# Row halves and marks for the down products and the output projection in the last sections of an attention and gated feed-forward kernel

## The chip, the cores and the metric

The kernel runs on one core of one Trainium2 chip. The metric is the device time of one execution in microseconds (us); of several executions the median is taken. The kernel before takes 2547.48 us, the median of 3 runs from 2546.96 to 2547.53 us.

## The reference

The input is 2048 tokens of width 576. With `xn` the layer norm of `x`, two branches are computed from `xn`: a 32-head attention (18 numbers a head) with its output projection `wo`, and a feed-forward branch with 4608 hidden values. They meet in the last line.

```python
x = A_x
xn = _layernorm(x, axis=-1)
s = _A_ref(xn, A_wqkv, A_wo)                     # softmax(q k^T) v, then @ wo
g = _silu(_B_ref(xn, B_w_gate, B_w_up, B_w_down))  # (gelu(xn @ w_gate) * (xn @ w_up)) @ w_down
return x + s * g
```

All arrays are 32-bit floats. The kernel splits every operand of a large product into a high and a low part and adds three products of parts (high by high, high by low, low by high).

## The kernel before, in words

**The whole.** A first stage norms `x`, transposes it and computes queries, keys and values. Then come 144 sections. One section computes 128 hidden values for 512 tokens: `gate_up` (L400 to L416) runs 27 pairs of products, and in each pair the gate product uses the rows 0 to 63 of the TensorE array (PE) and the up product the rows 64 to 127, at the same time. Two sections (g = 0 and 1) make one round r of 18; four blocks b of 512 tokens make 72 rounds. The sections 10 to 137 carry the attention between their products. The sections 138 to 143, which the loop variable of L939 counts as n = 128 to 133, belong to the last block (b = 3, rounds 15 to 17). They have no attention left; beside the feed-forward branch they carry the output projection. They are the place of the change.

**A last section, in PE's order.** PE's order is the order in which the program is written; it is not rearranged. First the 27 pairs of `gate_up`. Then the down products of half a round (`down`, L512): for two groups of 128 tokens (j) and two halves of the 576 columns (c), that is four sums, six products each (`DOWN`, L458), 128 rows deep and 288 columns wide. Then, for n = 129 to 132, the output projection of three places (a place is a block b and a group j, 16 in all): `project_o` (L899) makes two sums a place, 14 products each (`OUT`, L933), so 84 products. The last section, n = 133, has no projection in its loop body; two places follow at L986, then the down products of round 17, then the last two places.

**What the other engines do in a last section.** `activate` (L424): ScalarE (ACT) squares the gate sum (L426), VectorE (DVE) makes the inner part of the gelu (L427). `run_rest` (L554) then calls `rest` (L436): tanh on ACT (L437) and two products on DVE (L440, L444) that read the gate and up sums out of PSUM. `add_down` (L448) adds a finished down sum to `Y` in SBUF (DVE, L453). For every place, `gate_place` (L895) computes tanh on ACT (L420) and a product over 576 columns on DVE (L421); the tile `th` between them has one buffer. `put` (L905) multiplies a finished projection sum by the gate (L909, reads PSUM) and adds `x` (L910), both on DVE. `finish` (L566) with `cut` splits the hidden values and, when g is 1, the down weights: the high part on ACT (L116), the low part on DVE (L117). `prepare(p)` (L920) has GpSimd (POOL) split the attention output of place p into `oh` and `ol` (L106, L108) with a cast of 64 rows (L882), and loads `x` and the stored sums of that place. `AHEAD` is 3: the parts of place p use the buffers of place p - 3. POOL also splits the gate and up weights of the next section.

**What sets the order.** PSUM has eight banks in three groups: `BANKS` gives two to "f", three to "m" and three to "s". A sum holds one bank until it has been read. `gate_up` takes two of "f" or two of "m" in turn. The down sums and the projection sums of the last sections take "s" one after another. `kept` (L397) pins an instruction behind whatever instruction was written last for the same engine; from n = 128 on nearly all work of ACT, DVE, POOL and SyncE (SP) is pinned so. In the last sections the order on DVE is: L427, four `add_down`, L440, L444, then place by place gate and puts, with `finish` behind the second place.

**Halves and marks, as they stand.** In the attention sections `half_downs` (L474) runs a whole round of eight down sums in row halves: every product is two products of 64 rows, one for each half of the array, side by side. The two halves of one sum may not write its bank at the same time, so one half begins with the last two sums and the other with the first, and each sum changes halves: `behind` (L468) writes a one-column "mark" on ACT which waits for the last product of the first half, and the first product of the other half waits for the mark. `FF["rest"]` is then called from inside `half_downs`, behind a mark:

```python
if begun == 0 and i == 0 and k in seen:
    after(one, seen[k])
...
    seen[k] = behind(one)
    if k in (0, late) and FF["rest"]:
        FF["rest"].pop(0)(seen[k], evicted if k == 2 else None)
```

Of the kernel before, what the change touches and what calls it, by code (L numbers as in the profile page):

```python
# [8 lines left out]
F32 = mybir.dt.float32  # L9
# [8 lines left out]
P = 128  # L18
# [3 lines left out]
KT = 4  # L22
# [47 lines left out]
def kernel(ctx: ExitStack, tc: tile.TileContext, x, wqkv, wo, w_gate, w_up, w_down, out):  # L70
# [34 lines left out]
    def split(hi, lo, raw, keep=lambda i: i):  # L105
        first = nc.gpsimd.tensor_scalar(hi, raw, 1.0, 1.0, op0=ALU.mult, op1=ALU.mult)  # L106
        keep(first)
        low_part[:] = [keep(nc.gpsimd.tensor_tensor(lo, raw, f(hi), op=ALU.subtract))]  # L108
        return first
# [287 lines left out]
    def kept(i):  # L397

        if FF["keep"]:
            tc.keep_in_program_order(i)  # L400
        return i
# [58 lines left out]
    def bank(tag):  # L460
        return ps.tile([P, 288], F32, name="py", tag=tag, bufs=BANKS[tag])
# [9 lines left out]
        after(it, one)  # L471
        return it

    def half_downs(b, r, hs, wd, Y):  # L474

        m = len(DOWN)
        sums = [(j, c) for j in range(TB // P) for c in range(2)]
        low = len(sums) - 2  # L480
        pys, seen, evicted = {}, {}, None
        late = 2 if r == NR - 1 else 1

        def downs_of(a, ks):
            for k in ks:
                for i in range(m):
                    def step(k=k, i=i):
                        nonlocal evicted
                        j, c = sums[k]
                        fresh = k not in pys  # L490
                        if fresh:
                            pys[k] = bank("mmsmfmss"[k])
                        begun = a if k < low else 1 - a
                        one = down_product(pys[k], hs, wd, j, c, i, slice(HR * a, HR * a + HR), fresh,
                                           begun == 0 and i == m - 1)
                        if begun == 0 and i == 0 and k in seen:
                            after(one, seen[k])
                        if i == m - 1:
                            if begun == 0:
                                evicted = add_down(b, r, pys[k], Y, j, c)  # L500
                            elif a == 1:
                                seen[k] = behind(one)
                                if k in (0, late) and FF["rest"]:
                                    FF["rest"].pop(0)(seen[k], evicted if k == 2 else None)
                    yield step

        n = range(len(sums))
        rows = [*downs_of(0, n[low:]), *downs_of(0, n[:low])], [*downs_of(1, n)]
        for i, both in enumerate(zip(*rows, strict=True)):
            for half in both if i < low * m + m else both[::-1]:  # L510
                half()

    def down(b, r, hs, wd, Y, js, once):
        last = len(DOWN) - 1
        if once:
            if js[0] == 0:
                half_downs(b, r, hs, wd, Y)
        else:
            for j in js:
                for c in range(2):  # L520
                    py = bank("sf"[c if b == NB - 1 and r == NR - 1 else 0])
                    for i in range(len(DOWN)):
                        down_product(py, hs, wd, j, c, i, start=(i == 0), stop=(i == last))
                    add_down(b, r, py, Y, j, c)
        if b < NB - 1 and r == NR - 1:
            for j in js:
                kept(nc.sync.dma_start(ys[b * TB + j * P:b * TB + (j + 1) * P, :], Y[:, j]))
# [104 lines left out]
    def load_wo(i):  # L632

        for w, c, k in ((w, c, k) for w in range(2) for c in range(2) for k in range(NK)):
            if i != (5 + k // 3 if w and c else k) or (c and not w):
                continue
            n, wide = min(P, D - k * P), D if not w else 288
            to, cc = f(flat[i]), slice(288 * c, 288 * c + wide)
            o = D if w and not c else 288 * (k % 3) if w else 0
            for a in range(1 if w or n == P else 2):  # L640
                kept(nc.sync.dma_start(to[HR * a:HR * a + n, o:o + wide], wos[w, k * P:k * P + n, cc]))
            if w and n < P:
                kept(nc.gpsimd.memset(to[HR:P, o:o + wide], 0.0))

    with tc.tile_pool(name="att", bufs=1, reuse_waits="tile") as att:
# [211 lines left out]
    with tc.tile_pool(name="epi", bufs=1, reuse_waits="tile") as epi:  # L857
# [20 lines left out]
        def split_o(b, j):  # L878

            oh, ol = parts_of(b, j)  # L880
            split(oh, ol, OT[b % 2][:, :, j * P:(j + 1) * P], kept)
            kept(nc.gpsimd.tensor_copy(oh[HR:P, KT, :], ol[0:HR, KT, :]))  # L882

        def row_tile(name):
# [14 lines left out]
        def project_o(b, j, c, tag):  # L899
            po = ps.tile([P, TB], F32, name="po", tag=tag, bufs=BANKS[tag])[:, 0:288]  # L900
            for i, (k, x_, w) in enumerate(OUT):
                nc.tensor.matmul(po, parts_of(b, j)[x_][:, k, :], OW[w][c][k], start=(i == 0), stop=(i == len(OUT) - 1))  # L902
            return po

        def put(b, j, c, po, add):  # L905

            cc = slice(288 * c, 288 * c + 288)
            xx, yy = XY[b, j]
            kept(nc.vector.scalar_tensor_tensor(yy[:, cc], yy[:, cc], 0.25, po, op0=ALU.mult, op1=ALU.mult))  # L909
            kept(add.tensor_tensor(yy[:, cc], yy[:, cc], xx[:, cc], op=ALU.add))  # L910
            if c or b == NB - 1:
                cc = cc if b == NB - 1 else slice(0, D)
                kept(nc.sync.dma_start(out[b * TB + j * P:b * TB + (j + 1) * P, cc], yy[:, cc]))
# [6 lines left out]
        def prepare(p):  # L920

            if p < len(places):
                b, j = places[p]
                split_o(b, j)
                load_xy(b, j)
                if j == 0 and 0 < b < NB - 1:
                    load_o(b + 1)
# [10 lines left out]
        for n in range(NU * NA, ENDS):  # L938
            first, last = n == NU * NA, n == ENDS - 1  # L939
            if first:  # L940
                rec = epi.tile([P, D], F32, name="th")[:, 0:TB]
                tc.keep_in_program_order(nc.vector.reciprocal(rec, SUM))
            section([], "m" if n % 2 else "f", ahead=first)
            if first:
                FF["keep"] = True
                load_wo((n - 1) % KB)
                load_o(0)
                for o in OT:
                    kept(nc.gpsimd.memset(o[HR:P, KT, :], 0.0))
                prepare(0)  # L950
                prepare(1)
                next_weights(n)
                prepare(2)
                where = [(u % NQ, slice(S - TB, S)) for u in range(NU - 2, NU)]
                store_sums(*where[1])
                kept(nc.sync.dma_start(rT[H - QD:H, S - TB:S], rec.rearrange("(a p) t -> a p t", p=32)[:, 0, :]))
                pieces = [(S3[0:QD * DH, 0:TB], ffn.tile([P, TB], F32, name="t2", bufs=1)[0:QD * DH]),
                          [row_tile(m)[0:QD * DH, 0:TB] for m in ("xx", "yy")]]
                for piece, to in zip(pieces, where):
                    load_numbers(*piece, *to)  # L960
                load_o(1)
            else:
                next_weights(n)
                for k in range(0 if last else NG - 1):
                    split_gu(FF["w"], k, kept)
            downs()
            run_rest()
            if first or last:
                finish(epi, cut, 2)
            else:  # L970
                for i in range(3):
                    b, j = places[done]
                    if b < NB - 1:
                        gate_place(b, j)
                    for c in range(2):
                        put(b, j, c, project_o(b, j, c, "s"), nc.vector)
                    done += 1
                    if i == 0:
                        split_gu(FF["w"], NG - 1, kept)
                    prepare(done - 1 + AHEAD)  # L980
                    if i == 1:
                        finish(epi, cut, 2)
                    if done == 2:
                        for piece, to in zip(pieces, where):
                            norm_numbers(*piece, *to, nc.vector)
        for b, j in places[done:done + 2]:  # L986
            for c in range(2):
                kept(nc.scalar.activation(SS[2 * j + c], project_o(b, j, c, "s"), AF.Copy))
            done += 1
            prepare(done - 1 + AHEAD)  # L990
# [51 lines left out]
```

## Time and profile before

| what | value |
|---|---|
| time, median of 3 runs | 2547.48 us |
| span of the profiled execution, first to last instruction | 2545.4 us |
| busy: PE / DVE / ACT / POOL | 2538.4 / 1950.4 / 1555.1 / 1320.7 us |
| granted TensorE clock, mean | 1.000 |

One execution was profiled, and its own time is the span; the median of the runs is 2.08 us above it. Times in the views count from the first instruction. A row of a timeline has the start, the duration (merged rows: of all together), engine, line, operation, output and inputs, and how many instructions stand in it; in brackets the idle time before and what ended it. "64\*128 64x288" is a product of 64 rows by 288 columns in one half of the array; "x2" with that shape is a pair side by side. The chain of work that ended last lists start, duration and work without gaps. Matmuls overlap in the records: the rate is seen in the distance of their starts, not in their durations.

### The profile page before, as it was taken

The page shows a single profiled execution, that of the slowest core. Times are in us where ns is not written, and L with a number is a line of the kernel's source. Part 1 is how long each engine was busy: PE and PEld are TensorE (multiplying, and loading weights), DVE is VectorE, ACT ScalarE, POOL GpSimd, SP SyncE. Part 2 cuts the span into 40 slices and gives each one's busy share as a digit, 9 for nine tenths or more (in the row PEclk, how much of TensorE's full clock was granted, in tenths as well). Part 3 has the DMA queues.
Part 4 walks back from the last instruction along what each step waited for, and adds up shares of the span by engine and source line. Part 5 has one row for each costly group of instructions (what it writes and reads, how often), then busy time and mean ns, then how long its engine had stood idle before and what let it go on. Part 6 is the DMA issues. An engine that isn't in the chain of part 4 may idle for free.

```text
span 2545.4 us, 63167 instructions
## 1 busy us (share of the span) xinstructions
PE 2538.4 (100%) x23974; PEld 2008.4 (79%) x23974; DVE 1950.4 (77%) x3499; ACT 1555.1 (61%) x3050; POOL 1320.7 (52%) x1447
## 2 busy tenths in 40 slices
PE   9999999999999999999999999999999999999999
PEld 8888877777777777777777787777777777787798
DVE  5316988888888888888888888888888888887277
ACT  3223366666677666676666677666676666676612
POOL 2117545555465554445565545554446555455675
PEclk9999999999999999999999999999999999999999
DMA  8876444444465444444455444444446444444483
GB/s 267 269 241 158 100 103 106 100 111 109 107 150 121 104 109 112 113 112 110 111 125 140 116 111 106 105 108 112 109 109 153 115 109 109 108 106 99 114 242 107
DMA packets 398686, 325.51 MB, mean 128 GB/s; under 512 B 117408, under 2 KB 309184, under 8 KB 398384
## 3 DMA queue, kind: packets, MB, share of 16 engines
q1 hardware_dynamic: 398384, 321.47, 49.7%
q8 instruction: 191, 3.13, 0.5%
q14 instruction: 111, 0.91, 0.1%
HBM read 266.63 MB, written 54.70 MB: 126 GB/s over the span
## 4 chain that ended last, share of the span: by engine, by line
PE 98%; ACT 1%; DVE 0%; DMA 0%; SPq 0%; issue 0%; ACTq 0%
PE pg L413 29%; PE py L465 18%; PE acc L764 18%; PE pm L698 9%; PE pe L729 9%; PE po L180 7%; PE pu L413 6%; PE po L902 2%; ACT pT L730 1%; PE pt L241 0%; SPq L665 0%; DMA xx<-in_A_x_dram 0%; DVE bs L209 0%; ACT t L426 0%; DMA KS<-qk 0%
## 5 line engine op out<-in xcount | busy, mean ns | idle before, releaser
L730 ACT ACTIVATE pT<-pe 128x512 f32<-128x512 f32 x2048 | 1153.3, 598 | 368.7 <-PE pm L698 226.3
L699 DVE TENSOR_REDUCE mx<-pm 128x1 f32<-128x512 f32 x2048 | 1249.6, 680 | 151.3 <-PE pm L698 149.0
L413 PE MATMUL pg<-xd,wh 64*128 64x512 f32 x2592 | 928.9, 390 | 0.0
L413 PE MATMUL pu<-xd,wh 64*128 64x512 f32 x2592 | 928.6, 390 | 0.0
L698 PE MATMUL pm<-KS,q 64*128 64x512 f32 x2048 | 779.0, 388 | 0.8 <-DMA KS<-qk 0.5
L729 PE MATMUL pe<-q,KS 64*128 64x512 f32 x2048 | 775.2, 387 | 0.0
L413 PEld LDWEIGHTS pg<-xd,wh 64*128 64x128 f32 x2592 | 476.5, 184 | 115.9 <-POOL wh L106 21.1
L413 PE MATMUL pg<-xd,wl 64*128 64x512 f32 x1296 | 501.6, 387 | 0.0
L413 PE MATMUL pu<-xd,wl 64*128 64x512 f32 x1296 | 501.4, 387 | 0.0
L413 PEld LDWEIGHTS pu<-xd,wh 64*128 64x128 f32 x2592 | 477.0, 184 | 2.0
L764 PE MATMUL acc<-pT,VS 128*32 128x512 f32 x4096 | 452.8, 594 | 0.0
L108 POOL TENSOR_TENSOR wl<-raw,wh 128x384 fp32r<-128x384 f32 x432 | 434.2, 1019 | 13.7
L106 POOL TENSOR_SCALAR hh<-t 128x512 fp32r<-128x512 f32 x128 | 79.1, 618 | 652.0 <-DVE t L440 637.8
L698 PEld LDWEIGHTS pm<-KS,q 64*128 64x128 f32 x2048 | 374.2, 184 | 31.1 <-DVE mx L699 4.3
L729 PEld LDWEIGHTS pe<-q,KS 64*128 64x128 f32 x2048 | 370.9, 184 | 21.9
L465 PE MATMUL py<-dh,hh 64*128 64x288 f32 (+1 forms) x2160 | 360.3, 294 | 0.3
L465 PE MATMUL py<-dl,hh 64*128 64x288 f32 (+1 forms) x2160 | 358.7, 292 | 0.0
L465 PE MATMUL py<-dh,hl 64*128 64x288 f32 (+1 forms) x2160 | 358.3, 292 | 0.0
L764 PEld LDWEIGHTS acc<-pT,VS 128*32 128x32 f32 x4096 | 127.4, 110 | 289.9 <-issue 278.0
L106 POOL TENSOR_SCALAR wh<-raw 128x384 fp32r<-128x384 f32 x432 | 217.2, 515 | 143.7 <-PE pu L413 83.4
L453 DVE TENSOR_TENSOR Y<-py,Y 128x288 f32<-128x288 f32 x544 | 227.1, 452 | 59.8 <-PE py L465 52.7
L413 PEld LDWEIGHTS pg<-xd,wl 64*128 64x128 f32 x1296 | 238.7, 184 | 32.1
(119 smaller groups left out, 3106.7 us busy)
## 6 DMA issues: line engine op xcount, KB each, us to landing
KS<-qk SPq DMA_DIRECT2D x1536, 36.0 KB
raw<-in_B_w_gate_dram SPq DMA_DIRECT2D x144, 288.0 KB
raw<-in_B_w_up_dram SPq DMA_DIRECT2D x144, 288.0 KB
raw<-in_B_w_down_dram SPq DMA_DIRECT2D x67, 576.0 KB
VS<-vs SPq DMA_DIRECT2D x128, 152.0 KB
qk<-t SPq DMA_DIRECT2D x72, 256.0 KB
q<-qk SPq DMA_DIRECT2D x384, 36.0 KB
xx<-in_A_x_dram SPq DMA_DIRECT2D x32, 288.0 KB
```

The source lines that it names most:

```text
L106: first = nc.gpsimd.tensor_scalar(hi, raw, 1.0, 1.0, op0=ALU.mult, op1=ALU.mult)
L108: low_part[:] = [keep(nc.gpsimd.tensor_tensor(lo, raw, f(hi), op=ALU.subtract))]
L180: nc.tensor.matmul(o, st, m, start=(i == 0), stop=(i == len(terms) - 1))
L413: nc.tensor.matmul(o, w[1 + wp][k][rr, c, :], xd[xp][k][rr, c, :], start=(i == 0), stop=(i == len(terms) - 1))
L453: one = kept(nc.vector.tensor_tensor(yy, py, yy, op=ALU.add))
L465: return nc.tensor.matmul(py, hs[g][a][rr, j * P:(j + 1) * P], wd[w][rr, g, 288 * c:288 * c + 288], start=start, stop=stop)
L698: nc.tensor.matmul(pm, QS[u, r][rr, t * P:(t + 1) * P], KS[(u * NA + c) % KB][r][rr, :], start=True, stop=True)
L699: nc.vector.tensor_reduce(MX[u][:, 2 * r + a, t, c:c + 1], pm, axis=AX.X, op=ALU.max)
L729: nc.tensor.matmul(pe, KS[(u * NA + c) % KB][r][rr, t * P:(t + 1) * P], QS[u, r][rr, :], start=True, stop=True)
L730: nc.scalar.activation(PT[u, kt][:, 2 * r + a, :], pe, AF.Exp, scale=SCALE)
L764: nc.tensor.matmul(ACC[u][32 * a:32 * a + 32, :], VS[(u * NA + c) % VB][:, v:v + 32], pt[:, a, :], start=first, stop=last, skip_group_chec ...
L902: nc.tensor.matmul(po, parts_of(b, j)[x_][:, k, :], OW[w][c][k], start=(i == 0), stop=(i == len(OUT) - 1))
```

## The change

The down products of the last sections, except round 17, go through `half_downs` with four sums (two groups of tokens) in the banks "smss"; all four sums now get marks. `project_o` in the sections n = 129 to 132 is replaced by `project_row`, which runs the six sums of three places in row halves in the same manner, in the banks "ffmsss" or "mmmsss". The 64 remaining rows of `wo` (the fifth part, `KT`) no longer need two products of full depth: with one more cast on POOL and one more load of weight rows, a sum has 13 or 14 products in each half in place of 14 of full depth; the six sums have 81 in each half in place of 84. What followed a sum in program order (`gate_place`, `put`, `finish`, `prepare`) now follows from `added`, which is called where a sum's last product is written.

```diff
-    def half_downs(b, r, hs, wd, Y):
+    def half_downs(b, r, hs, wd, Y, js, banks):
         m = len(DOWN)
-        sums = [(j, c) for j in range(TB // P) for c in range(2)]
+        sums = [(j, c) for j in js for c in range(2)]
...
-                            pys[k] = bank("mmsmfmss"[k])
+                            pys[k] = bank(banks[k])
...
-                            elif a == 1:
+                            elif a == 1 or len(sums) == 4:
                                 seen[k] = behind(one)
...
             if js[0] == 0:
-                half_downs(b, r, hs, wd, Y)
+                half_downs(b, r, hs, wd, Y, range(TB // P), "mmsmfmss")
+        elif b == NB - 1 and r < NR - 1:
+            half_downs(b, r, hs, wd, Y, js, "smss")
...
-            for a in range(1 if w or n == P else 2):
+            for a in range(1 if n == P or w and not c else 2):
                 kept(nc.sync.dma_start(to[HR * a:HR * a + n, o:o + wide], wos[w, k * P:k * P + n, cc]))
-            if w and n < P:
+            if w and not c and n < P:
                 kept(nc.gpsimd.memset(to[HR:P, o:o + wide], 0.0))
...
             split(oh, ol, OT[b % 2][:, :, j * P:(j + 1) * P], kept)
+            kept(nc.gpsimd.tensor_copy(ol[HR:P, KT, :], oh[0:HR, KT, :]))
             kept(nc.gpsimd.tensor_copy(oh[HR:P, KT, :], ol[0:HR, KT, :]))
...
+        LAST = [[[(KT, 0, 0), (KT, 0, 1)], [(KT, 0, 0)]], [[(KT, 0, 0)], [(KT, 0, 0), (KT, 1, 1)]]]
+
+        def project_row(first, banks, added):
+            jobs = [(*places[first + i], c) for i in range(3) for c in range(2)]
+            n = len(jobs)
+            pos, seen = {}, {}
+            def sums_of(a, ks):
+                for k in ks:
+                    b, j, c = jobs[k]
+                    terms = OUT[:3 * KT] + LAST[c][a]
+                    begins = (k < n - 2) == (a == 1)
+                    for i, (p, x_, w) in enumerate(terms):
+                        def step(k=k, b=b, j=j, c=c, i=i, p=p, x_=x_, w=w, last=i == len(terms) - 1, begins=begins):
+                            if begins and i == 0:
+                                pos[k] = ps.tile([P, TB], F32, name="po", tag=banks[k], bufs=BANKS[banks[k]])[:, 0:288]
+                            rr = slice(HR * a, HR * a + HR)
+                            one = nc.tensor.matmul(pos[k], parts_of(b, j)[x_][rr, p, :], OW[w][c][p][rr, :],
+                                                   start=begins and i == 0, stop=last and not begins)
+                            if not begins and i == 0:
+                                after(one, seen[k])
+                            if last and begins:
+                                seen[k] = behind(one)
+                            elif last:
+                                added(k // 2, c, pos[k])
+                        yield step
+            for both in zip(sums_of(0, [n - 2, n - 1, *range(n - 2)]), sums_of(1, range(n)), strict=True):
+                for half in both:
+                    half()
...
-                for i in range(3):
-                    b, j = places[done]
-                    if b < NB - 1:
+                def added(i, c, po, first=done, n=n):
+                    b, j = places[first + i]
+                    if c == 0 and b < NB - 1:
                         gate_place(b, j)
-                    for c in range(2):
-                        put(b, j, c, project_o(b, j, c, "s"), nc.vector)
-                    done += 1
+                    put(b, j, c, po, nc.vector)
+                    if c == 0:
+                        return
                     if i == 0:
                         split_gu(FF["w"], NG - 1, kept)
-                    prepare(done - 1 + AHEAD)
+                    prepare(first + i + AHEAD)
                     if i == 1:
                         finish(epi, cut, 2)
-                    if done == 2:
+                    if first + i == 1:
                         for piece, to in zip(pieces, where):
                             norm_numbers(*piece, *to, nc.vector)
+
+                project_row(done, "ffmsss" if n % 2 else "mmmsss", added)
+                done += 3
```

## The prediction on record

> **What bounds the kernel now.** I read the page first: its span, and the chain of work that ended last.
>
> ```profile
> span 2545.4 us, 63167 instructions
> PE 98%; ACT 1%; DVE 0%; DMA 0%; SPq 0%; issue 0%; ACTq 0%
> ```
>
> The last columns of the chain are all PE: the kernel is as long as PE's own program. So an edit of PE's program counts in full, and any wait put into it counts in full too. The profiled execution took 2545.4 us; the median of the runs is 2.08 us above it. I work in the trace and add the difference to the median. Next the chain in order of time, in the last sections.
>
> ```profile
> 2437.04 11.09 PE po L902 x84
> 2448.13 0.43 PE pg L413
> 2448.56 0.23 PE pg L413
> ...
> 2454.48 3.38 PE py L465 x24
> 2457.86 11.10 PE po L902 x84
> ```
>
> The reader sees one section: 84 projection products (0.132 us each), 27 gate and up pairs, 24 down products. The section repeats after 2457.86 - 2437.04 = 20.82 us. The first pair behind the full-depth products takes 0.43 where the others take 0.23, and the 24 down products take 3.38 where 24 x 0.132 is 3.17: every change between full depth and 64-row halves costs 0.20 us. Third, who else is close behind PE: the busy times in the projection of n = 130 (columns: window and length, then PE, PEld, DVE, ACT, POOL).
>
> ```profile
> 2457.70:2468.80 11.10, 11.10 (x86) 11.03 (x84) 10.30 (x15) 1.90 (x3) 6.99 (x7) 1.00 1.02 297
> ```
>
> DVE is busy for 10.30 of 11.10 us. It is not on the chain, but it has almost no room: what makes DVE wait there comes back as time later. **This is the row that decides my forecast.**
>
> **What the change takes away.** Halves run in this kernel already, in the attention sections:
>
> ```profile
> 2336.89 0.29 PE L465 MATMUL py<-dh,hl 64*128 64x288 f32 x2
> ...
> 2337.68 0.30 PE L465 MATMUL py<-dh,hl 64*128 64x288 f32 x2
> ```
>
> Six pairs start in 0.79 us, 0.132 a pair: a pair of halves costs what one full-depth product costs. So splitting by itself gains nothing, and two things remain. (1) Products: 81 pairs for 84 products, in four sections: 12 x 0.132 = 1.6 us. (2) Changes of depth: n = 128 to 132 lose two each (in front of the down products and behind the full-depth part), n = 133 only moves one: 10 x 0.20 = 2.0 us. Together -3.6 us.
>
> The Trainium skill, "TensorEngine Tiling (Array Packing)", Overview, counts a contraction of at most 64 rows as what row tiling speeds up; here 128 rows are filled, and the trace agrees with 0.132 against 0.132. The same page, Key Properties, says that a change of tiling mode drains the array; the trace agrees with 0.20 us. By that page alone the sum would be (2) and, where only 64 rows are left, (1).
>
> **What it adds at the end of the down products.** The marks first. In the trace a mark starts 0.39 us after the start of the product that it waits for (2337.28 against 2336.89) and lasts 0.20; PE waited for one hardly ever:
>
> ```profile
> PEld py L465 <- ACT mark L470: 0.6, 2, 0.3
> ```
>
> With four sums there are six pair steps (0.79 us) between the last product of a sum's first half and the first of its second, and two marks stand behind each other: 0 to 0.35 us a time. I take 0 at the first change and 0.3 at the second, where ACT's tanh stands in front of the marks. In the projection 14 or 15 steps (1.9 us) lie between; I take 0.
>
> The order on DVE weighs more. `half_downs` calls `rest` behind the first mark, so L440 and L444, which wait for tanh, are pinned in front of the four `add_down`. The attention sections show this order already, L440 and then the sums:
>
> ```profile
> 2368.97 0.69 DVE L440 SCALAR_TENSOR_TENSOR t<-t,t 128x512 f32<-128x512 f32 x1
> 2369.58 1.25 DVE L453 TENSOR_TENSOR Y<-py,Y 128x288 f32<-128x288 f32 x3
> ```
>
> In the last sections the adds went first. And "smss" gives three of the four sums the three "s" banks, of which the first projection sum (k = 4, "s") needs one at once. So the projection can't start before the first add is done. I count from A, the start of L427:
>
> ```profile
> 2337.28 0.20 ACT L470 ACTIVATE mark<-mark 128x1 f32<-128x1 f32 x1
> ...
> 2435.10 0.64 ACT L437 ACTIVATE t<-t 128x512 f32<-128x512 f32 x1 [0.75 <-DVE t L427]
> 2435.64 0.67 ACT L420 ACTIVATE th<-yy 128x576 f32<-128x576 f32 x1
> ```
>
> ```profile
> 2434.38 0.69 DVE L427 SCALAR_TENSOR_TENSOR t<-t,pg 128x512 f32<-128x512 f32 x1 [3.17 <-ACT t L426]
> ...
> 2437.45 0.68 DVE L440 SCALAR_TENSOR_TENSOR t<-t,pg 128x512 f32<-128x512 f32 x1
> 2438.16 0.69 DVE L444 TENSOR_TENSOR t<-t,pu 128x512 f32<-128x512 f32 x1
> 2438.76 0.75 DVE L421 SCALAR_TENSOR_TENSOR yy<-th,yy 128x576 f32<-128x576 f32 x1
> ```
>
> A is 2434.38; tanh ends at 2435.74, A + 1.36. L440 follows at 1.39, L444 0.71 later, the first add 0.60 later, at A + 2.70; an add takes 0.42 to 0.5 (1.25 for three) and PE follows at A + 3.2. Before:
>
> ```profile
> 2436.87 0.42 PE L902 MATMUL po<-KS,oh 128*128 128x288 f32 x2
> ```
>
> that is A + 2.49. So (3): +0.7 us ahead of each projection, in n = 129 to 133. The 0.3 of the marks lies inside it, except in n = 128, where no projection follows. If the bank that is taken is that of the second add, 0.45 more each.
>
> **What it adds in the projection.** Let R be the start of a projection. Before, the tanh of the first gate ran ahead of it (2435.64). Now it is written at step 40 of 81, where the first sum ends, and is pinned on ACT behind the mark of the sum k = 2, whose product is step 39. ACT is blocked in order: mark at R + 39 x 0.132 + 0.39 = R + 5.5, tanh from R + 5.7 to R + 6.4 (0.67). On DVE the first gate product is pinned behind the last add, at about R + 1.3; **so DVE stands idle for 5 us of a section in which it had under 1 us to spare.** Behind it wait the puts, the other gates (`th` has one buffer), the split in `finish`, and then L427 of the next section.
>
> When does DVE come free? Gates and puts of the first place took 2441.78 - 2438.76 = 3.0 us, so the second gate is issued at R + 9.4. There POOL's split of the next place is running, as it was for the second gate before:
>
> ```profile
> 2440.83 0.72 POOL L106 TENSOR_SCALAR oh<-OT 128x640 fp32r<-128x640 f32 x1 [4.60 <-PE po L902]
> ...
> 2453.06 0.40 POOL L882 CAST oh<-ol 64x128 fp32r<-64x128 f32 x1
> ```
>
> ```profile
> 2441.78 2.12 DVE L421 SCALAR_TENSOR_TENSOR yy<-th,yy 128x576 f32<-128x576 f32 x1
> ...
> 2453.71 0.65 DVE L910 TENSOR_TENSOR yy<-yy,xx 128x288 f32<-128x288 f32 x1
> 2455.14 0.69 DVE L427 SCALAR_TENSOR_TENSOR t<-t,pg 128x512 f32<-128x512 f32 x1 [0.78 <-ACT t L426]
> ...
> 2462.61 2.12 DVE L421 SCALAR_TENSOR_TENSOR yy<-th,yy 128x576 f32<-128x576 f32 x1
> ...
> 2470.87 1.34 DVE L910 TENSOR_TENSOR yy<-yy,xx 128x288 f32<-128x288 f32 x1
> ...
> 2483.45 2.12 DVE L421 SCALAR_TENSOR_TENSOR yy<-th,yy 128x576 f32<-128x576 f32 x1
> ...
> 2494.18 0.66 DVE L910 TENSOR_TENSOR yy<-yy,xx 128x288 f32<-128x288 f32 x1
> ```
>
> The second gate took 2.12 where the first took 0.75 with POOL idle, and ended 3.07 us after POOL's split began (2443.90 - 2440.83). Now that split is released by step 53: R + 53 x 0.132 + 0.4 = R + 7.4, and the gate ends at R + 10.5. From there to DVE's last put the same work remains, in another order (second place and first changed about): 10.46 us in n = 129 (2443.90 to 2454.36), 7.48 in 130, 9.27 in 131, and 132 is like 130. One more cast a split on POOL: nothing to 0.70 us (a longer wait of DVE) twice a section; I take 0.3 a section, near the 0.40 of the row. DVE is free at R + 21.3, 18.3, 20.1, 18.3.
>
> PE would let L427 start earlier. Before it started at 2455.14, R + 18.27; three products (0.40) and a change of depth (0.20) go: R + 17.67. So (4): DVE is late by 3.6, 0.6, 2.4 and 0.6, **7.3 us**, and what follows L427 (tanh, L440, L444, first add, projection) moves with it. Where DVE keeps up, a section takes 17.67 + 3.2 = 20.87 in place of 20.82, +0.2 for four.
>
> The Trainium skill, "SBUF — State Buffer", Who interferes with whom, says that a DVE instruction with two SBUF inputs and a GpSimd one that reads SBUF exclude each other for a whole instruction. The 2.12 against 0.75 agrees. By that rule the waits stay in the new order, as (4) takes them.
>
> Costed at nothing: the splits of POOL (three took 12.6 us; from R + 7.4, with three added casts of 0.7, done by R + 22.1, and the next projection, which now reads the third place's parts in its first step, starts at R + 20.9 at the earliest and at R + 24.5 behind n = 129, the section where POOL took 12.6; uncovered it would cost at most 1.2); the added load of weight rows in place of a memset, sections ahead of its use; SP's stores and loads, which move back with the puts by about 5 us and are read a section later.
>
> **The sum.** n = 128: two changes of depth gone, 0.3 for marks: -0.1. First projection +0.7. Four sections +0.2 and +7.3. Behind the start of the last projection nothing changes. Together +8.1: 2547.5 + 8.1 = **2555.6 us**.
>
> **The rivals.** *DVE keeps up.* The place is DVE's work behind the second gate; it decides at R + 17.67, that is if 7.2 us suffice. For it: without POOL beside it DVE's products are much shorter (0.75 for 2.12). Against it: 10.46, 7.48 and 9.27 in the rows, and POOL's work falls into the same stretch. Then (4) is 0 and +0.8 remains: 2548.3, not slower by anything that can be told. *PE alone counts:* also (3) vanishes, because the first add is done early. For it: 3.6 us are surely saved. Against it: the pinned order. 2543.9. *Longer:* the second add's bank (5 x 0.45 = 2.2), casts of 0.7 twice a section (4 x 1.1 = 4.4): 2555.6 + 6.6 = 2562.2. *The halves don't run side by side:* 324 + 144 more products of 0.132, 62 us: 2609; the pairs at 2336.89 speak against it.
>
> **Chances.** My forecast 0.58, DVE keeps up (wholly or in part) 0.20, longer 0.12, PE alone 0.08, not side by side 0.02. 0.2% is 5.1 us, about what a measurement of this kernel can tell from no change. Slower than 2552.6: 0.58 + 0.12 + 0.02 = 0.72; within: 0.26, with the greater part of PE alone; faster than 2542.4: 0.02, if PE alone gains more than I count. The range from 2548.0 to 2562.2 leaves out PE alone, half of "longer" and the last case: 0.16.
>
> **What would show it.** Right: DVE idle for about 5 us in front of the first gate product of a section; L440 and L444 ahead of the four adds; PE waiting for DVE at the first projection product; L427 waiting for no ACT but following DVE's last put, in n = 130 and 132 above all. Wrong: tanh of the first gate early in the projection; gate products of 0.75; sections of 20.4 us; PE waits for marks of over 0.5 us, or for POOL's parts, which my sum leaves out.

## The result, and the profile after

| kernel | median, us | lowest and highest | executions |
|---|---|---|---|
| before | 2547.48 | 2546.96 to 2547.57 | 5 |
| after | 2560.86 | 2559.83 to 2562.05 | 5 |

The ratio is 1.0053, with a 95% interval of 1.0042 to 1.0064. The change makes the kernel 13.4 us slower; the prediction was 8.1 us slower. The time lies inside the range. The profiled execution of after took 2562.05 us itself, the highest of the five.

The page of after, span and chain:

```profile
span 2560.0 us, 64185 instructions
...
PE 95%; DVE 2%; ACT 1%; issue 1%; DMA 1%; SPq 1%; POOL 0%; DVEq 0%; ACTq 0%
```

PE had 98% of the chain before and has 95% now; DVE went from nothing to 2%. The chain in order of time shows where DVE and ACT came in (start, duration, what). It is the section from the first product of the projection of n = 129 to that of n = 130:

```profile
2438.45 5.66 PE po L926 x81
...
2444.20 0.68 ACT th L420
...
2456.08 0.77 DVE hl L117
...
2460.93 4.69 PE py L465 x36
2465.62 5.91 PE po L926 x70
```

PE leads for 5.66 us, until the mark of k = 2. From there to 2460.93 the chain is tanh, gates, puts, splits and the two products for the numbers of the norm (L610), with short gaps between: DVE work that before ran unseen beside the products. The chain comes back to PE only in the down products. In PE's timeline the projection of n = 129 starts at 2438.45 and that of n = 130 at 2465.42, so this section takes 26.97 us; before, every one took 20.83 (2457.86 - 2437.04 in the rows of the prediction, to 0.01).

The timeline of DVE for the same stretch (start, duration, line, operation, shapes, idle time before and what ended it):

```profile
2435.11 0.69 DVE L427 SCALAR_TENSOR_TENSOR t<-t,pg 128x512 f32<-128x512 f32 x1 [4.25 <-ACT t L426]
2436.50 0.69 DVE L440 SCALAR_TENSOR_TENSOR t<-t,pg 128x512 f32<-128x512 f32 x1 [0.70 <-ACT t L437]
2437.29 0.69 DVE L444 TENSOR_TENSOR t<-t,pu 128x512 f32<-128x512 f32 x1
2437.89 1.54 DVE L453 TENSOR_TENSOR Y<-py,Y 128x288 f32<-128x288 f32 x4
2444.91 0.76 DVE L421 SCALAR_TENSOR_TENSOR yy<-th,yy 128x576 f32<-128x576 f32 x1 [5.47 <-ACT th L420]
...
2447.35 1.35 DVE L945 TENSOR_TENSOR yy<-yy,xx 128x288 f32<-128x288 f32 x1
2448.62 0.84 DVE L421 SCALAR_TENSOR_TENSOR yy<-th,yy 128x576 f32<-128x576 f32 x1
...
2450.78 2.12 DVE L421 SCALAR_TENSOR_TENSOR yy<-th,yy 128x576 f32<-128x576 f32 x1
...
2460.91 0.46 DVE L945 TENSOR_TENSOR yy<-yy,xx 128x288 f32<-128x288 f32 x1
2461.29 0.68 DVE L427 SCALAR_TENSOR_TENSOR t<-t,pg 128x512 f32<-128x512 f32 x1
```

L440 and L444 stand ahead of the four adds. Behind the adds DVE is idle for 5.47 us. At the end L427 has no wait in brackets: it follows DVE's last put.

The four sections, with R for the start of a projection and A for the start of L427 ahead of it:

| section | from R to the next A, forecast | measured | from A to R, forecast | measured |
|---|---|---|---|---|
| n = 129 to 130 | 21.3 | 22.84 | 3.2 | 4.13 |
| n = 130 to 131 | 18.3 | 19.81 | 3.2 | 3.37 |
| n = 131 to 132 | 20.1 | 20.40 | 3.2 | 3.37 |
| n = 132 to the last | 18.3 | 19.04 | 3.2 | 3.38 |
| sum | 78.0 | 82.09 | 12.8 | 14.25 |

Before, the same sums were 4 x 18.27 = 73.1 and 4 x 2.56 = 10.2. So the profile's 14.6 us (2560.0 - 2545.4) divide into 9.0 behind the starts of the projections and 4.0 ahead of them in these sections, 0.9 ahead of the first projection (3.34 for 2.49), and 0.7 that stand before L427 of n = 129 already (2435.11 - 2434.38 = 0.73 in the quoted rows). That last item is hardly work of the change. 0.82 stood already at L427 of n = 128 (2425.44 against 2424.62), and the section n = 128 then took 9.67 instead of 9.76, the -0.1 of the forecast. `fill_gap`, an experiment below whose program is that of after up to n = 130, has 2434.41 where after has 2435.11.

### The profile page after: what moved, and what is told of

It reads as the page before. It is cut to its first block, busy times and chain, and to the rows that moved or that the text cites. A ratio compares the mean times of both kernels' runs of the same rounds, so it can differ in the third digit from the quotient of the medians.

```text
span 2560.0 us, 64185 instructions
## 1 busy us (share of the span) xinstructions
PE 2541.2 (99%) x24430; PEld 2000.2 (78%) x24430; DVE 1953.5 (76%) x3499; ACT 1563.9 (61%) x3098; POOL 1326.3 (52%) x1462
## 4 chain that ended last, share of the span: by engine, by line
PE 95%; DVE 2%; ACT 1%; issue 1%; DMA 1%; SPq 1%; POOL 0%; DVEq 0%; ACTq 0%
PE pg L413 27%; PE acc L766 18%; PE py L465 17%; PE pm L700 9%; PE pe L731 9%; PE po L180 7%; PE pu L413 6%; PE po L926 1%; PE po L905 1%; ACT pT L732 1%; DVE yy L421 1%; DVE yy L945 1%; DVE yy L944 0%; PE pt L241 0%; SPq L667 0%
## 5 line engine op out<-in xcount | busy, mean ns | idle before, releaser
L108 POOL TENSOR_TENSOR wl<-raw,wh 128x384 fp32r<-128x384 f32 x432 | 434.9, 1020 | 13.7
```

## The experiments

The question was which of the two forecast terms holds, what the other 5 us are, and whether the order or the company of POOL makes DVE late. The theory: the order (term 3) costs 0.8 ahead of each projection, and DVE's idle time (term 4), lengthened by POOL's splits beside it, costs the rest. The rivals: the halves themselves or their marks are slow; or DVE's idle time is harmless and only POOL, or only the order, counts.

**Down products alone.** Before, with the four sums of the last sections in halves; the projection stays as it was.

```diff
...
+        elif b == NB - 1 and r < NR - 1:
+            half_downs(b, r, hs, wd, Y, js, "smss")
...
```

> Only the down products go in halves; the projection stays in full-depth products with its old order. Theory (order on DVE): the two products behind tanh stand in front of the four adds, so each of five projections starts about 0.86 us later (3.35 us behind the start of L427 in place of 2.49), and n = 128 gives about -0.1: 2551.7 us, 2550.5 to 2553. DVE is not idle in front of the first gate, so no more is lost. Rival (the projection row alone makes the loss): 2547.5 or a little less.

Measured 2552.19 against 2547.72 us on the same chip, ratio 1.0018 (1.0009 to 1.0027): 4.5 us slower. From A to R it takes 3.33 to 3.38 in all five sections; from R to the next A 18.34 or 18.35, where before took 18.27. Waits of PE (who waited for what, total, times, longest):

```profile
PE po L904 <- DVE Y L453: 1.8, 3, 0.6
```

Term (3) stands, and alone it is a little larger than I took it: 0.8 us a section, in which PE's first projection product waits for the adds behind L440 and L444.

**The row alone.** After, with the down products at full depth as before.

```diff
...
-        elif b == NB - 1 and r < NR - 1:
-            half_downs(b, r, hs, wd, Y, js, "smss")
...
```

> Only the projection goes in halves with the new place of gates, puts, finish and prepare; the down products stay as they were. Theory (DVE idle until the first sum ends, its work done late): from projection start to L427 of the next section about 22.8, 19.8, 20.4 and 19.0 us in place of 18.3, so about +9 us: 2556.5, and down to 2554.5 if the clock does not fall as it did in the changed kernel. Rival (the banks and the adds in front of the projection make the loss): 2546 us, the 1.6 us of the twelve products saved.

Measured 2555.92, ratio 1.0032 (1.0019 to 1.0044): 8.2 us slower than the 2547.72 of before and near the expectation. The idle time of DVE is there without the halves of the down products:

```profile
2443.79 0.76 DVE L421 SCALAR_TENSOR_TENSOR yy<-th,yy 128x576 f32<-128x576 f32 x1 [4.59 <-ACT th L420]
```

From R to the next A: 22.89, 19.26, 20.45, 19.09, nearly as in after. From A to R it takes 1.99 to 2.58, but 4.05 in n = 132, where the granted clock fell. The two parts give 4.5 + 8.2 = 12.7 of the 13.4 us: they nearly add up, and neither part alone is faster than before.

**Adds ahead of `rest` again.** After, but with four sums `rest` is no longer called from within the down products, so L440 and L444 follow the adds.

```diff
-                                if k in (0, late) and FF["rest"]:
+                                if k in (0, late) and FF["rest"] and len(sums) > 4:
```

> The changed kernel, but with four sums the two products behind tanh are written behind the four adds, as before. Theory: the first add, and with it the projection and all that hangs on its steps, comes about 0.85 us earlier in five sections: 2560.9 - 4.2 = 2556.7 us. Rival (only the amount of work on DVE counts, not its order): no change, 2560 to 2561.

Measured 2557.61, ratio 1.0038 (1.0025 to 1.0050): 3.25 us less than after, where 4.2 was expected. From A to R: 2.34, 4.14, 1.95, 3.97, 2.27. Three of five are 1.0 to 1.4 us shorter, and so term (3) is the order of L440, L444 and the adds. In the two sections of about 4 us (n = 130 and 132) the granted clock fell to 0.50, in after only in n = 130; more on that below.

**The first gate ahead of the row.** After, with the first place's tanh and gate written ahead of the projection.

```diff
-                    if c == 0 and b < NB - 1:
+                    if c == 0 and i and b < NB - 1:
                         gate_place(b, j)
...
+                gate_place(*places[done])
                 project_row(done, "ffmsss" if n % 2 else "mmmsss", added)
```

> The changed kernel, but the first gate of a row (tanh and its product on DVE) is written ahead of the row instead of at the end of its first sum. Theory (DVE idle): the gate product falls into DVE's idle time, the puts start about 1.5 us earlier in four sections; 2560.9 - 5.6 = 2555.3 us, 2553 to 2556.5. Rival (DVE's collisions with POOL set the end of its work, wherever it starts): 2560, within 1 us of the changed kernel.

Measured 2558.86, ratio 1.0043 (1.0031 to 1.0056): only 2.0 us less than after, where 5.6 was expected. DVE's timeline in n = 129, and POOL's split beside it:

```profile
2444.07 0.46 DVE L944 SCALAR_TENSOR_TENSOR yy<-yy,po 128x288 f32<-128x288 f32 x1 [4.02 <-PE po L926]
...
2446.80 2.13 DVE L421 SCALAR_TENSOR_TENSOR yy<-th,yy 128x576 f32<-128x576 f32 x1
```

```profile
2446.65 1.67 POOL L108 TENSOR_TENSOR ol<-OT,oh 128x640 fp32r<-128x640 f32 x1
```

Half of my expectation failed. The gate is gone from behind the mark, but DVE then has nothing that it may do: it waits 4.02 us for the first sum. And the second gate, which comes earlier now, meets POOL's L108 and takes 2.13 instead of 0.84. So "the first gate behind a mark" was too narrow a name for the cause. In halves the first sum of a row ends half way through it (step 40 of 81), where it ended after 14 of 84 products before, and all of DVE's work that stands behind this sum comes late.

**Without POOL's splits in the row.** After, with the split and the casts of the attention outputs of the places 3 to 14 left out; the projection then uses the parts of earlier places.

```diff
-                split_o(b, j)
+                if not AHEAD <= p < 15:
+                    split_o(b, j)
```

> The changed kernel without POOL's splits and casts of the attention output for the places 3 to 14; the projection then uses the parts of earlier places, and that part of the computation is left out. Theory (DVE's late work is stretched by POOL's splits beside it): gate products of 0.75 and sums with x of 0.46 us throughout, DVE done by 15 to 17.7 us behind the start of a projection and so in time; what remains is 3.35 for 2.49 us in front of each projection: 2549.0 us. Rival (the late start of DVE's work alone makes the loss, POOL does not matter): 2559 to 2561.

Measured 2551.23 against 2547.65, ratio 1.0013 (1.0005 to 1.0022): 9.6 us less than after, with DVE's order untouched; 2549.0 was expected. From R to the next A: 18.87, 17.80, 17.98, 17.81, where 17.67 was forecast as PE's own pace; from A to R 3.28 to 3.34. The same groups of DVE in the last sections of three kernels; first before, then after, then without the splits (line, shapes, count, busy, mean ns of one, idle time ahead):

```profile
L910 DVE TENSOR_TENSOR yy<-yy,xx 128x288 f32<-128x288 f32 x24 | 15.2, 634 | 0.8
L421 DVE SCALAR_TENSOR_TENSOR yy<-th,yy 128x576 f32<-128x576 f32 x12 | 15.2, 1264 | 0.0
L909 DVE SCALAR_TENSOR_TENSOR yy<-yy,po 128x288 f32<-128x288 f32 x24 | 10.8, 451 | 2.1 <-PE po L902 0.8
L117 DVE TENSOR_TENSOR hl<-t,hh 128x512 fp32r<-128x512 f32 x4 | 8.2, 2055 | 0.0
```

```profile
L945 DVE TENSOR_TENSOR yy<-yy,xx 128x288 f32<-128x288 f32 x24 | 22.1, 919 | 0.8
L421 DVE SCALAR_TENSOR_TENSOR yy<-th,yy 128x576 f32<-128x576 f32 x12 | 14.9, 1239 | 22.4 <-ACT th L420 22.4
L944 DVE SCALAR_TENSOR_TENSOR yy<-yy,po 128x288 f32<-128x288 f32 x24 | 10.8, 448 | 1.2
...
L117 DVE TENSOR_TENSOR hl<-t,hh 128x512 fp32r<-128x512 f32 x4 | 3.1, 772 | 0.0
```

```profile
L945 DVE TENSOR_TENSOR yy<-yy,xx 128x288 f32<-128x288 f32 x24 | 13.3, 553 | 0.8
...
L421 DVE SCALAR_TENSOR_TENSOR yy<-th,yy 128x576 f32<-128x576 f32 x12 | 10.2, 847 | 21.8 <-ACT th L420 21.8
...
L117 DVE TENSOR_TENSOR hl<-t,hh 128x512 fp32r<-128x512 f32 x4 | 4.4, 1092 | 0.0
```

The idle time stays at 21.8 us, and yet DVE nearly keeps up (1.2 us late in n = 129, 0.1 to 0.3 in the others): its products are shorter. They are not at 0.75 and 0.46 throughout, as expected, because POOL's split of the weights remains and moves into their way: in n = 129 and 130 `hl` took 1.50 beside it. Between before and after the stretched time didn't grow much, it moved: sums with x, gates and `hl` took 38.6 us together before and 40.1 after. The split `hl` lost 5.1 us, because it now comes behind POOL's last L108 of a row, beside two casts, and the 24 sums with x gained 6.9. The puts (L909, L944), which read one operand out of PSUM, hold 451 and 448 ns in both. The Trainium skill, "SBUF — State Buffer", Who interferes with whom, ties the exclusion to two SBUF operands; the steady 448 to 451 ns and the 919 against 553 agree.

**Something for PE to do in the gap.** After, with ten products of 64 rows into a sum that nobody reads, ahead of the down products of n = 130, to see whether the granted clock then stays up.

```diff
+            if n == NU * NA + 2:
+                pz = ps.tile([P, TB], F32, name="pz", tag="m", bufs=3)
+                hz = FF["down"][0][2][0][0]
+                for _ in range(10):
+                    nc.tensor.matmul(pz, hz[0:HR, 0:P], hz[0:HR, :], start=True, stop=True)
             downs()
```

> The changed kernel with ten added products (64 rows by 512 columns, their sum is not read, about 2.3 us) between the gate and up pairs and the down products of n = 130, where PE stood idle for 2.56 us and the granted clock then fell to 0.50 for about 6.5 us. Theory (the idle time of PE lowers the clock, at a price of about 1.6 us): the clock stays at 1.00 there, 2559.3 us. Rival (the clock falls for another reason, or the products come on top): 2560.9 to 2563.

Measured 2560.42, ratio 1.0052 (1.0039 to 1.0064): within the interval of after's ratio. The clock fell all the same. The windows of after in n = 130, then those of this kernel behind the filled gap (columns: window, length, busy PE, PEld, DVE, ACT, POOL, granted clock, DMA share, GB/s):

```profile
2457.00:2458.00 1.00, 0.00 (x0) 0.00 (x0) 1.00 (x1) 0.00 (x0) 0.91 (x1) 1.00 0.94 320
...
2460.00:2461.00 1.00, 0.07 (x2) 0.07 (x2) 0.97 (x3) 0.00 (x0) 0.92 (x2) 0.50 0.94 240
...
2466.00:2467.00 1.00, 1.00 (x14) 1.00 (x12) 0.48 (x2) 0.00 (x0) 0.00 (x0) 0.59 1.01 390
```

```profile
2459.00:2460.00 1.00, 0.00 (x0) 0.00 (x0) 1.00 (x2) 0.00 (x0) 1.00 (x2) 0.77 0.94 258
2460.00:2461.00 1.00, 0.76 (x6) 0.76 (x8) 0.96 (x3) 0.00 (x0) 0.92 (x2) 0.50 0.91 277
```

So the first gap (2.56 us in after) isn't by itself what lowers the clock: here the products left 0.32 us of it idle, and with the later stretch of 1.73 us the clock fell as before. The products used one half of the array only; whether that matters wasn't tried. The total can't price the fall either, because in this execution the clock fell in n = 132 too, behind an idle stretch of 2.46 us.

**More work ahead of the row.** Adds first, first and second gate ahead of the row (from n = 130 on), and `finish` behind the first place instead of the second. The second tanh goes into the tile S3.

```diff
-                    if i == 1:
+                    if i == 0:
                         finish(epi, cut, 2)
...
+                gate_place(*places[done])
+                if done:
+                    gate_place(*places[done + 1], S3[:, 0:D])
                 project_row(done, "ffmsss" if n % 2 else "mmmsss", added)
```

> The changed kernel with the products behind tanh behind the adds, the first gate (and for n of 130 and above the second) written ahead of the row, and finish behind the first place. Theory (order on DVE): the work that is left behind the first sum ends 1 to 3.5 us late in n = 129 and 131 and hardly late in the others: 2549.5 us, 2547 to 2553. Rival (collisions with POOL eat what the order gives): 2556.

Measured 2554.25, ratio 1.0024 (1.0014 to 1.0034), 4.8 us over the expectation. My edit brought a wait of its own. ACT's timeline and PE's waits in n = 130:

```profile
2467.06 0.68 ACT L420 ACTIVATE S<-yy 128x576 f32<-128x576 f32 x1 [6.87 <-DMA oN<-S]
```

```profile
PE po L926 <- ACT mark L470: 4.0, 1, 4.0
```

S3 was still being stored, tanh waited 6.87 us for it, the marks stood behind tanh on ACT, and PE behind the marks. In the two sections without that wait, n = 131 and 132, R to the next A is 17.76, with POOL at work as ever.

The same without POOL's splits of the places 3 to 14:

```diff
-                split_o(b, j)
+                if not AHEAD <= p < 15:
+                    split_o(b, j)
```

> As all_early, without POOL's splits and casts of the attention output for the places 3 to 14 (that part is left out). Theory: DVE keeps up everywhere, and the twelve products and ten changes of depth are all that is left of the change: 2547.6 - 3.6 = 2544 us. Rival (the pairs or the marks cost something themselves): 2547 or more.

Measured 2550.64, ratio 1.0012 (1.0003 to 1.0021), 6.6 us over the expectation. The same wait of my edit, 3.8 us of PE's time, stood in n = 130 (23.35 from R to the next A). The total mixes this wait with what was asked; n = 131 and 132 (17.70, 17.71) are what they were with the splits.

**The same with free tiles.** The second tanh in two pieces of 288 columns, into tiles that are free by then, in all four sections; the numbers of the norm (two small DVE jobs) go ahead of the row of n = 130. The edit is shown against the kernel of "More work ahead of the row", without the lines for the norm.

```diff
...
+        def gate_halves(b, j):
+            yy = XY[b, j][1]
+            for c, th in enumerate((SUM[:, 0:288], S3[:, 576:864])):
+                cc = slice(288 * c, 288 * c + 288)
+                gate(yy[:, cc], th, yy[:, cc])
...
                 gate_place(*places[done])
-                if done:
-                    gate_place(*places[done + 1], S3[:, 0:D])
+                gate_halves(*places[done + 1])
...
```

> As all_early, but the second gate is written ahead of the row in all four sections (in two pieces whose tanh goes to tiles that nothing holds), and the two products for the last attention heads stand ahead of the row of n = 130. Theory (order on DVE): from projection start to L427 17.8 us in all four sections as all_early had it in n = 131 and 132, 2.4 from L427 to the projection, the clock at 1.00: 2547.6 - 3.2 = 2544.4 us, 2543.5 to 2546. Rival (a loss of the change that lies in the pairs, the marks or the added casts remains): 2547 or more.

Measured 2544.61 (11 executions, 2543.96 to 2546.42) against 2547.66, ratio 0.9988 (0.9979 to 0.9997): 3.05 us less than before, 16 less than after. The interval excludes no change only just, and the difference is below the 0.2% that I set as the limit; the trace is plainer. The chain in order of time:

```profile
2436.29 10.76 PE po L932 x162
...
2456.43 10.82 PE po L932 x162
...
2476.60 10.83 PE po L932 x162
```

A section takes 20.14 and 20.17 us (2456.43 - 2436.29, 2476.60 - 2456.43), 0.65 to 0.7 less than before; PE waits for nobody in the last sections. R to the next A is 17.72 to 17.76. The halves, the marks and the added casts are all still in this kernel, so the rival that they are slow themselves falls, but for the 0.5 us by which the gain stays under the forecast 3.6. DVE starts the row with three gate products where after had 5.47 us of idle time:

```profile
2438.38 0.75 DVE L421 SCALAR_TENSOR_TENSOR yy<-th,yy 128x576 f32<-128x576 f32 x1
2439.05 0.45 DVE L421 SCALAR_TENSOR_TENSOR yy<-accs,yy 128x288 f32<-128x288 f32 x1
2439.42 0.45 DVE L421 SCALAR_TENSOR_TENSOR yy<-S,yy 128x288 f32<-128x288 f32 x1
```

**What the 81 pairs are worth.** That kernel with 84 pairs a row, 14 products in every half.

```diff
-        LAST = [[[(KT, 0, 0), (KT, 0, 1)], [(KT, 0, 0)]], [[(KT, 0, 0)], [(KT, 0, 0), (KT, 1, 1)]]]
+        LAST = [[[(KT, 0, 0), (KT, 0, 1)]] * 2] * 2
```

> As early_two, with 14 products in both halves of every sum, so 84 pairs a row in place of 81. Theory: 12 pairs of 0.132 us more, 1.6 us above early_two. Rival (PE is not what bounds these sections): no more than 0.5 us above it.

Measured 2548.85, ratio 1.0006 (0.9997 to 1.0015): 4.2 us more than with 81, where 1.6 was expected. R to the next A: 19.39, 18.16, 21.77, 18.16. In n = 130 and 132 the row costs 0.40 more, which is 3 x 0.132. In the other two the edit does more than its size: the sums k = 2 and k = 4 now end in the same step, so the puts stand in another order, and the third gate meets POOL's split again in n = 129 and 131 and takes 2.12. The row of n = 129 has no other wait and takes 1.2 us more than those of n = 130 and 132. In n = 131 tanh also waits for a load, in ACT's timeline:

```profile
2483.97 0.44 ACT L420 ACTIVATE accs<-yy 128x288 f32<-128x288 f32 x1 [2.14 <-DMA yy<-ys]
```

Term (1) is confirmed by the two sections without such waits; the total is not a measure of it.

## Why the prediction was right, and where its size was off

**Direction and mechanism.** Right: what the change saves is real but small, and DVE, with little room, is made to wait at the head of the row and comes late at its end. DVE's idle time was forecast at about 5 us and was 5.47. That DVE keeps up, and that PE alone counts, both fell with 13.4 us. The time is nearest to the rival "longer" (2562.2), but not by its causes: the second add's bank and the long casts are not on the chain. That the range held the time is in part luck, because its upper end stood there for those causes. And the halves do run side by side (81 pairs in 10.76 us where nothing waits).

**Gains, -3.6.** Borne out for the most part where nothing covers them: with the work ahead of the row the kernel is 3.05 us faster than before, and 3 pairs cost 0.40 a row.

**Term (3), ahead of the projections.** Forecast 0.7 a section, 3.2 from A to R. Measured 3.37 and 3.38 where the clock held, and 3.33 to 3.38 with the down products alone. It is the order: with the adds first again, 2.34, 1.95 and 2.27.

**Term (4), the mis-sized one.** Forecast 7.3 (3.6, 0.6, 2.4, 0.6). From R to the next A, the four sections were 4.1 us longer than forecast: 1.5, 1.5, 0.3, 0.7. In n = 129 the first gate came at R + 6.46 (forecast 6.4). The step that failed is "so the second gate is issued at R + 9.4", with "the gate ends at R + 10.5". One sum with x was stretched to 1.35 ahead of it, it was issued at R + 10.17, took only 0.84 and ended at R + 11.01. And that from there "the same work remains" failed too: the third gate took 2.12. (In DVE's order the third place's gate comes before the second's, not the second's before the first's: of the sums behind the first place, k = 4 ends one step before k = 2.) POOL's timeline in after shows why the hit changed place:

```profile
2446.73 1.65 POOL L108 TENSOR_TENSOR ol<-OT,oh 128x640 fp32r<-128x640 f32 x1
2448.45 0.40 POOL L884 CAST ol<-oh 64x128 fp32r<-64x128 f32 x1
2448.80 0.82 POOL L885 CAST oh<-ol 64x128 fp32r<-64x128 f32 x1
...
2450.63 1.65 POOL L108 TENSOR_TENSOR ol<-OT,oh 128x640 fp32r<-128x640 f32 x1
```

The second gate (2448.62) stood beside two casts, the third (2450.78) beside L108, and the sum at 2447.35 beside the L108 before it. In all four sections the sums with x took 919 ns on average for 634; in n = 129 DVE was free at R + 22.8. I had moved a stretch of DVE's timeline as a block. It can't be moved so, because which operation is stretched depends on what of POOL's stands beside it at that moment.

**What the sum didn't have.** DVE late also means `dl` late and the banks of the last sums occupied, so PE stood in the down products (total, times, longest):

```profile
PE py L465 <- DVE dl L117: 5.0, 2, 2.6
PE py L465 <- DVE yy L944: 3.3, 3, 1.7
...
PE py L465 <- ACT mark L470: 0.2, 1, 0.2
```

Most of this lies beside DVE's own lateness and costs nothing on top, but in n = 130 the granted clock fell to 0.50 behind it, for 6 to 7 us. The 18 pairs of down products left then ran at 0.24 us instead of 0.132, as the starts in PE's timeline show:

```profile
2462.06 0.44 PE L465 MATMUL py<-dl,hh 64*128 64x288 f32 x2
2462.30 0.44 PE L465 MATMUL py<-dh,hl 64*128 64x288 f32 x2
```

From A to R it took 4.13 instead of 3.37, so 0.8 us ahead of the projection, and about 0.5 behind its start (an estimate from some five pairs at 0.24): 1.3 of the 5 us that were missing. Why the clock fell there stays open. Marks cost 0.2 us once, and PE never waited for POOL's parts, as forecast.

**One cause or two.** Neither DVE's late start nor POOL's splits do it alone. Without the splits the late start costs 0.1 to 1.2 us a section. With the work ahead of the row the splits cost at most 0.1 (17.72 to 17.76 against the forecast 17.67), but only in that order: with 84 pairs, where the puts come in another order, DVE was 1.2 late again in n = 129. Together they cost 1.4 to 5.2 (19.04 and 22.84 against 17.67). What stays open is how much of the difference between executions of after is the fallen clock, since one was profiled.

## What to carry to other kernels

When an edit changes the step at which sums end in one engine's order, look at what is written behind those sums for the other engines: here three gates, six puts and a split stood behind a sum that ends half way through the row. Write what needs no sum ahead of the long row, into tiles that are truly free at that time. An engine that is busy for 10.30 of 11.10 us has no such wait to give away, and the work behind the wait is not to be shifted as a block if its durations depend on a neighbour.

## What the runs showed of the hardware

In these runs the granted clock fell to 0.50 behind idle stretches of PE of little over 2 us, for which the forecast had no term. With the first gate ahead of the row it fell in n = 132 after a single stretch in which PE was idle for 2.30 us (windows; the stretch ends in the second row):

```profile
2504.00:2505.00 1.00, 0.00 (x0) 0.00 (x0) 1.00 (x2) 0.00 (x0) 1.00 (x1) 0.96 1.07 295
2505.00:2506.00 1.00, 0.93 (x8) 0.94 (x10) 0.97 (x4) 0.00 (x0) 0.92 (x2) 0.50 0.90 334
```

In after, an idle stretch of 2.41 us at the same place in n = 132 (PE's timeline) left it at 1.00 (windows):

```profile
2508.27 0.40 PE L465 MATMUL py<-dl,hh 64*128 64x288 f32 x2 [2.41 <-DVE dl L117]
```

```profile
2508.00:2509.00 1.00, 0.73 (x10) 0.73 (x12) 0.97 (x4) 0.00 (x0) 0.92 (x2) 1.00 0.91 302
```

With the filled gap, where the program around n = 132 is that of after, it fell behind 2.46 us. So length alone doesn't decide in these runs. The Trainium skill, "TensorE: Matmul & The Clock Gate", Part 1, gives a free-running window of about 3.4 us with half the clock behind an idle one, and in its part "HAM oscillation" warns of idle gaps longer than that; the granted clock of 0.50 agrees, the 2.30 us don't agree with that limit, and what exactly the condition is stays open here.
